# One core, three stages: q and k transposed by 64x64 products, one engine for the transposed x, and one-column result rows

## The chip, the cores and the metric

The kernel runs on one core of one Trainium2 chip. Its time is the device's time of one execution in microseconds (us); lower is better. Beside plain runs there is one profiled execution, from which the trace comes.

## The reference

Three computations follow each other. Everything is float32.

```python
# 1. attention in chunks of 64: batch 8, heads 8, sequence 576, head size 64
scores = (1 / sqrt(64)) * q_c @ k_c.T          # 64x64 per chunk and head
attn   = exp(scores - max); attn /= (sum + 1e-9)
x      = attn @ v_c                            # as 4608 tokens of 512
# 2. one expert of 8 for each token, chosen by normalized x against the experts' embeddings
logits = xn @ en.T / tau;  e = argmax(logits);  gate = softmax(logits)[e]
x      = gate * (relu(x @ w1[e]) @ w2[e])      # 512 -> 1024 -> 512
# 3. a gated layer
h = x @ w_in;  out = (h * sigmoid(1.702 * h)) @ w_out    # 512 -> 2048 -> 512
```

## The kernel before

The order of the work is written out by hand: each engine runs its instructions in the order in which the program issues them, and waits are put in where data or a buffer is needed. There is no planner.

**Attention loop.** 36 tiles of 128 tokens. `n` counts iterations (loop near the end of the first half, up to `n = 38`), and the stages of one tile are spread over several iterations. q and k are loaded by SyncE in units of 256 tokens (`load_qk`, 18 units, five buffers for k and four for q); v comes in 64 loads with three buffers of a batch each. In iteration n, in this order: `emit_T` transposes one unit of k or q on TensorE and returns the copies from PSUM to SBUF, which ScalarE makes; ScalarE squares x of tile n-3 (`emit_sq`); TensorE transposes the 16-bit pair of x of tile n-5 (`emit_XT`), forms the scores of tile n (`emit_S`); VectorE takes their maximum and subtracts it (`max_S`); `evac_XT` copies the transposed x out of PSUM, by ScalarE for odd tiles and from tile 30 on, by VectorE for the other even ones; `emit_X` forms the 16-bit pair of x of tile n-3 in one of three buffers, and SyncE stores it to `xs`; then come the transposed weights (`emit_PT`), the product with v (`emit_PV`) of tile n-2, the exponential (`exp_S`) and the division (`emit_x`). Between these, `drip(1)` issues one more VectorE step of the gate of an earlier batch of tiles (`norm`, `gate`, `order`, `tables`), and the logits of an earlier tile go ahead of the scores. The stores to `xs` and the loads of q, k and v stand in one queue, SyncE's, in the order of the program.

**Gate and slots.** The gate's last batch ends after the loop. `order` finds the tokens of the first three slots of 128 tokens, `tables` and `find_tokens`, `find_scales` those of all. `scale_of` builds each token's scale as the bits of a float (`sc_i`) from three looked-up parts.

**Experts.** 39 slots of 128 tokens: gather (`fetch`), DMA transpose (`turn`), `mm1` with a relu that ScalarE (high half) and VectorE (low half) make, `mm2`, then `mm2_evac`. At a change of expert `swap` splits new weights on ScalarE and VectorE; `load_next` loads the next ones. In the order of each engine `mm2_evac` of a slot follows the swap of w2, and the relu of the next slot follows it. `mm2_evac` squares the result on ScalarE with the sum per row, and VectorE makes from the sum a power of two that brings the row into the range of a 16-bit pair, and joins it with the token's scale; ScalarE then writes the high half of y, VectorE the low half, and four 32-bit words behind each row carry the token's number twice and its scale twice. Beside it `big_split` prepares the weights of stage 3 on VectorE, ScalarE and GpSimd.

**Gated layer.** Nine groups of 512 tokens, from about 672 us to the end; the diff does not touch it.

Of the kernel before, what the change touches and what calls it, by code (L numbers as in the profile page):

```python
# [9 lines left out]
F32 = mybir.dt.float32  # L10
F16 = mybir.dt.float16
BF16 = mybir.dt.bfloat16
I32 = mybir.dt.int32
U32 = mybir.dt.uint32
AF = mybir.ActivationFunctionType
ALU = mybir.AluOpType
# [8 lines left out]
BIAS = 127  # L25
# [3 lines left out]
EXP_BITS = 0x7F800000  # L29
MAN_BITS = 0x007FFFFF  # L30
# [4 lines left out]
def kernel(  # L35
# [13 lines left out]
    nc = tc.nc  # L49
    B, H, S, D = q.shape  # L50
    NT, DM = out.shape
# [4 lines left out]
    HP = H // 2  # L56
# [5 lines left out]
    MAXT = NTILE + NE - 1  # L62
# [7 lines left out]
    const = ctx.enter_context(tc.tile_pool(name="const", bufs=1))  # L70
# [4 lines left out]
    ps = ctx.enter_context(tc.tile_pool(name="ps", bufs=1, space=PSUM))  # L75
# [9 lines left out]
    YP = 2 * DM + 8  # L85
# [9 lines left out]
    identF = const.tile([128, 128], F32, name="identF")  # L95
# [5 lines left out]
    QR = QU // 128  # L101
# [27 lines left out]
    for b in range(B):  # L129
        for h in range(H):  # L130
            hp, h2 = divmod(h, 2)
# [20 lines left out]
    for t in vt:  # L152
# [15 lines left out]
        out=tri16, in_=ones16, pattern=[[1, 128]], compare_op=ALU.is_gt, fill=0.0,  # L168
# [19 lines left out]
    for m_, op_ in ((lt_m, ALU.is_lt), (le_m, ALU.is_le)):  # L188
        nc.vector.tensor_tensor(
            out=m_, in0=io_e.unsqueeze(1).to_broadcast([128, NE, NE]),  # L190
            in1=io_e.unsqueeze(2).to_broadcast([128, NE, NE]), op=op_,
# [15 lines left out]
    )  # L207
    id_i = const.tile([128, MAXT], I32, name="id_i")
    sc_i = const.tile([128, MAXT], I32, name="sc_i")

    tau_sb = const.tile([128, 1], F32, name="tau_sb")
    nc.scalar.dma_start(out=tau_sb, in_=tau.partition_broadcast(128))
# [121 lines left out]
    qkT = {}  # L334

    def emit_T(u, nm):

        src = raw.pop((u, nm))
        qkT[u, nm] = att.tile([128, HP, QU], F32, tag=nm + "T", name=nm + "T", bufs=2)
        evacs = []  # L340
        for h2 in range(2):
            p = ps.tile([128, HP, 128], F32, tag="A", name="tp", bufs=2)
            for hp in range(HP):
                nc.tensor.transpose(  # L344
                    p[:, hp, :], src[:, 2 * hp + h2].rearrange("p r d -> p (r d)"), identF
                )
            dst = qkT[u, nm][h2 * 64:(h2 + 1) * 64].rearrange("p hp (c r) -> p hp r c", r=QR)
            evacs.append([
                lambda r=r, p=p, dst=dst: nc.scalar.activation(  # L349
                    out=dst[:, :, r], in_=p[r * 64:(r + 1) * 64], func=AF.Copy  # L350
                )
                for r in range(2)
            ])
        return evacs

# [6 lines left out]
    xtp = sp2[:, :, HP * CH:512].bitcast(F16).rearrange("p a (c k) -> p a c k", k=128)  # L362
# [107 lines left out]
    def evac_XT(t):  # L470
        xT = att.tile([128, 2 * KD, 128], F16, tag="xTa", name="xTa", bufs=2)
        xv = xT.rearrange("p (a c) k -> p a c k", a=2)
        if t >= 30 or t % 2:
            nc.scalar.activation(out=xv, in_=xtp, func=AF.Copy)
        else:
            nc.vector.tensor_copy(xv, xtp)
        xT_t[t] = xT

    batches = [(0, 8), (8, 8), (16, 8), (24, 6), (30, 6)]
# [65 lines left out]
    def scale_of(cols, got, parts_i):  # L545
        nc.vector.tensor_copy(parts_i[:, 0], got[:, 0])
        nc.vector.scalar_tensor_tensor(
            out=parts_i[:, 1], in0=got[:, 1], scalar=1024.0, in1=got[:, 2], op0=ALU.mult, op1=ALU.add
        )
        nc.vector.scalar_tensor_tensor(  # L550
            out=sc_i[:, cols], in0=parts_i[:, 0], scalar=21, in1=parts_i[:, 1],
            op0=ALU.logical_shift_left, op1=ALU.bitwise_or
        )

    def gate(bi):
# [327 lines left out]
    def reg(ap, engines, hi):  # L883
        return nc.values_load(ap, engines=engines, min_val=0, max_val=hi)
# [163 lines left out]
    def mm2(i):  # L1048
        mm2_part(i, 0, KF)
        mm2_evac(i)  # L1050
# [15 lines left out]
    def mm2_evac(i):  # L1066
        hT_t.pop(i)
        p = py_t.pop(i)
        y = mo.tile([128, YP], F16, tag="y", name="y", bufs=2)
        ysq = mo.tile([128, DM], F16, tag="ysq", name="ysq", bufs=1)  # L1070
        s = mo.tile([128, 4], F32, tag="ys", name="ysc", bufs=2)
        si = s.bitcast(I32)
        c_i = sc_i[:, i:i + 1]
        tail = y[:, 2 * DM:YP].bitcast(I32).rearrange("p (a two) -> p a two", two=2)
        n = (YP - 2 * DM) // 4
        nc.scalar.activation(out=ysq, in_=p, func=AF.Square, scale=2.0 ** -20, accum_out=s[:, 0:1])
        nc.vector.tensor_scalar(si[:, 3:4], c_i, EXP_BITS, None, op0=ALU.bitwise_and)
        nc.vector.tensor_copy(tail[:, :, 0], id_i[:, i:i + 1].to_broadcast([128, n]))
        nc.vector.tensor_scalar(s[:, 0:1], s[:, 0:1], Y_MIN * 2.0 ** -40, None, op0=ALU.max)
        nc.vector.tensor_scalar(  # L1080
            si[:, 1:2], si[:, 0:1], 24, 23, op0=ALU.logical_shift_right, op1=ALU.logical_shift_left
        )
        nc.vector.tensor_scalar(
            si[:, 1:2], si[:, 1:2], -1.0, float((BIAS + Y_TOP - 20) << 23), op0=ALU.mult, op1=ALU.add
        )
        nc.vector.scalar_tensor_tensor(  # L1086
            out=si[:, 2:3], in0=c_i, scalar=MAN_BITS, in1=si[:, 1:2], op0=ALU.bitwise_and, op1=ALU.bitwise_or
        )
        nc.scalar.activation(out=y[:, 0:DM], in_=p, func=AF.Copy, scale=s[:, 2:3])  # L1089
        nc.vector.scalar_tensor_tensor(  # L1090
            out=y[:, DM:2 * DM], in0=p, scalar=s[:, 2:3], in1=y[:, 0:DM], op0=ALU.mult, op1=ALU.subtract
        )
        nc.vector.scalar_tensor_tensor(
            out=tail[:, :, 1], in0=si[:, 3:4].to_broadcast([128, n]), scalar=float(BIAS << 23),
            in1=si[:, 1:2].to_broadcast([128, n]), op0=ALU.add, op1=ALU.subtract,
        )
        if i < NSURE:
            nc.sync.dma_start(out=ys[i * 128:(i + 1) * 128, :], in_=y)
        elif i < SURE:
            row = reg(idx_y[0:1, i:i + 1], [ENG.SP], NT)  # L1100
            nc.sync.dma_start(out=ys[bass.ds(row, 128), :], in_=y)
        else:
            nc.gpsimd.indirect_dma_start(
                out=ys[:, :], out_offset=bass.IndirectOffsetOnAxis(ap=idx_y[:, i:i + 1], axis=0),
                in_=y[:, :], in_offset=None,
            )
# [8 lines left out]
    for nm in ("ku", "qu"):  # L1115
        for e in emit_T(0, nm):
            for f in e:
                f()
# [24 lines left out]
    for n in range(NTILE + 3):  # L1143
        rate[0] = 2 if 29 <= n < 33 else 1
        u, step = n // QR + 1, n % QR
        ev = [[], []]
        if u < NQ:
            ev = emit_T(u, "ku" if step == 0 else "qu")
            load(2 if n in (5, 9, 13, 17) else 1)
# [8 lines left out]
        if n - 1 in back:  # L1158
            evac_XT(back[n - 1])
            turned.append(back[n - 1])  # L1160
# [4 lines left out]
        if n in front:  # L1165
            evac_XT(front[n])
            turned.append(front[n])
# [31 lines left out]
        if n == NTILE + 2:  # L1199
            evac_XT(NTILE - 1)  # L1200
# [26 lines left out]
    swap(NSURE, 1)  # L1227
    steps(99)
    mm2_evac(1)
    turn(4)  # L1230
    fetch(5)
# [609 lines left out]
```

## Time and profile before

| | |
|---|---|
| runs | 1352.38, 1353.53, 1356.58 us; median 1353.53 |
| profiled execution | 1351.38 us, span 1349.4 us, mean granted clock 0.976 |
| TensorE (PE) busy | 1246.7 us (92%) |
| VectorE (DVE) busy | 1048.0 us (78%) |
| ScalarE (ACT) busy | 732.8 us (54%) |
| GpSimd (POOL) busy | 718.4 us (53%) |

The page divides the span into 40 slices of 33.7 us; a digit is the busy share in tenths, and PEclk the clock that TensorE was granted, in tenths:

```profile
PE   6777767899999999999899999999999999999997
DVE  4688888878988778886678696968687896968681
ACT  7899855235544545554463645545454645455452
PEclk9999877999999999999999999999999999999999
DMA  9999635668665759885507162544526062534413
```

The attention loop fills the first six or seven slices, the experts those up to the twentieth, the gated layer the rest. Busy shares are means over stages with different limits. "L349" is line 349 of the kernel; "<-" in a row's brackets tells what ended the wait ahead of it. PEld is TensorE's weight load, which runs beside its products.

### The profile page before, as it was taken

The page shows a single profiled execution, that of the slowest core. Times are in us where ns is not written, and L with a number is a line of the kernel's source. Part 1 is how long each engine was busy: PE and PEld are TensorE (multiplying, and loading weights), DVE is VectorE, ACT ScalarE, POOL GpSimd, SP SyncE. Part 2 cuts the span into 40 slices and gives each one's busy share as a digit, 9 for nine tenths or more (in the row PEclk, how much of TensorE's full clock was granted, in tenths as well). Part 3 has the DMA queues.
Part 4 walks back from the last instruction along what each step waited for, and adds up shares of the span by engine and source line. Part 5 has one row for each costly group of instructions (what it writes and reads, how often), then busy time and mean ns, then how long its engine had stood idle before and what let it go on. Part 6 is the DMA issues. An engine that isn't in the chain of part 4 may idle for free. (4 is left out here: it accounts for less than half of the span.)

```text
span 1349.4 us, 35343 instructions
## 1 busy us (share of the span) xinstructions
PE 1246.7 (92%) x14192; PEld 1027.2 (76%) x14192; DVE 1048.0 (78%) x1872; ACT 732.8 (54%) x1301; POOL 718.4 (53%) x652
## 2 busy tenths in 40 slices
PE   6777767899999999999899999999999999999997
PEld 4666656677676666667588888888888888888886
DVE  4688888878988778886678696968687896968681
ACT  7899855235544545554463645545454645455452
POOL 1455543142444254543167575757667675757664
PEclk9999877999999999999999999999999999999999
DMA  9999635668665759885507162544526062534413
GB/s 197 233 242 230 160 129 131 181 181 229 191 182 174 212 161 274 266 253 133 151 15 212 58 183 99 129 154 94 188 39 226 19 205 77 157 125 125 157 42 116
DMA packets 218454, 213.62 MB, mean 158 GB/s; under 512 B 127320, under 2 KB 171352, under 8 KB 218272
## 3 DMA queue, kind: packets, MB, share of 16 engines
q1 hardware_dynamic: 204880, 184.17, 51.0%
q0 software_dynamic: 6000, 19.67, 4.3%
q10 hardware_dynamic: 7392, 7.36, 1.6%
q8 instruction: 114, 1.87, 0.6%
q14 instruction: 68, 0.56, 0.2%
HBM read 154.98 MB, written 36.52 MB: 142 GB/s over the span
## 5 line engine op out<-in xcount | busy, mean ns | idle before, releaser
L1536 PEld LDWEIGHTS <-wS 128*128 128x128 f16 x3024 | 296.2, 98 | 48.9 <-issue 9.7
L1029 PEld LDWEIGHTS <-w1HL 128*128 128x128 f16 x3744 | 216.9, 99 | 24.1 <-DVEq L962 6.7
L1029 PE MATMUL ph<-xTm,w1HL 128*128 128x128 f16 x3744 | 223.0, 222 | 12.2 <-DVEq L962 5.5
L1064 PE MATMUL py<-w2HL,hT 128*128 128x512 f16 x912 | 203.9, 379 | 6.0 <-DVEq L962 3.4
L1064 PEld LDWEIGHTS <-hT 128*128 128x128 f16 x936 | 89.9, 98 | 109.1 <-issue 8.0
L1089 ACT ACTIVATE y<-py,ysc 128x512 f16<-128x512 f32 x38 | 26.1, 687 | 142.8 <-DVE ysc L1086 142.8
L1004 POOL DMA_INDIRECT xg<-xs,id_i x39 | 44.3, 1135 | 107.6 <-DMA xTm<-xg 70.0
L1536 PEld LDWEIGHTS <-w2HL 128*128 128x128 f16 x864 | 84.6, 98 | 10.6
L1536 PEld LDWEIGHTS <-w1HL 128*128 128x128 f16 x864 | 84.5, 98 | 9.8
L454 POOL TENSOR_TENSOR x<-x,sx_all 128x512 f32<-128x512 f32 x33 | 34.3, 1039 | 107.3 <-DVE rd L424 41.9
L1256 POOL TENSOR_TENSOR wS<-d_f,wS 128x512 f16<-128x512 f32 x28 | 37.0, 1339 | 73.4 <-ACT wS L1255 44.5
L1562 ACT ACTIVATE zA<-zA 128x512 f32<-128x512 f32 x72 | 45.3, 628 | 53.2 <-DVE zA L1559 26.9
L1403 POOL TENSOR_TENSOR w1HL<-zA,w1HL 128x512 f16<-128x512 f32 x36 | 48.5, 1346 | 43.6 <-ACT w1HL L1399 39.7
L1396 DVE TENSOR_TENSOR zA<-zA 128x512 f32<-128x512 f32 x72 | 65.6, 910 | 1.2
L1037 DVE SCALAR_TENSOR_TENSOR hT<-ph,hT 128x512 f16<-128x512 f32 x78 | 51.4, 684 | 14.8 <-ACT hT L1036 14.7
L1036 ACT ACTIVATE hT<-ph 128x512 f16<-128x512 f32 x78 | 44.2, 594 | 30.0 <-PE ph L1029 30.0
L1536 PE MATMUL pd<-stg,wS 128*128 128x256 f16 x456 | 54.5, 272 | 2.2 <-ACT stgB L1399 2.2
L1697 POOL DMA_INDIRECT out_dram<-hT,idc x36 | 35.4, 983 | 35.7 <-ACT hT L1692 32.6
L1536 PE MATMUL pa<-stg,wS 128*128 128x256 f16 x432 | 51.7, 273 | 1.5 <-ACT stgB L1399 1.5
L1090 DVE SCALAR_TENSOR_TENSOR y<-py,ysc,y 128x512 f16<-128x512 f32 x38 | 28.5, 751 | 28.8 <-ACT y L1089 28.8
L1536 PE MATMUL pb<-stg,wS 128*128 128x256 f16 x408 | 48.9, 272 | 1.5 <-ACT stgB L1399 1.5
L349 ACT ACTIVATE kuT<-tp 64x512 f32<-64x512 f32 x72 | 45.2, 628 | 8.8 <-PE tp L344 7.9
(408 smaller groups left out, 3134.4 us busy)
## 6 DMA issues: line engine op xcount, KB each, us to landing
ring<-wod SPq DMA_DIRECT2D x63, 1024.0 KB, 5.1
stg<-in_moe_w_dram SPq DMA_DIRECT2D x14, 1024.0 KB, 6.9
stgB<-in_moe_w_dram SPq DMA_DIRECT2D x14, 1024.0 KB, 6.8
ys<-y SPq DMA_DIRECT2D x39, 258.0 KB, 3.2
vt<-in_v_dram SPq DMA_DIRECT2D x64, 144.0 KB, 5.7
xs<-xr SPq DMA_DIRECT2D x36, 256.0 KB, 5.6
raw_o<-in_moe_w_in_dram SPq DMA_DIRECT2D x16, 512.0 KB, 4.3
raw_o<-in_moe_w_out_dram SPq DMA_DIRECT2D x16, 512.0 KB, 3.8
```

What stands on the lines that cost most here:

```text
L349: lambda r=r, p=p, dst=dst: nc.scalar.activation(out=dst[:, :, r], in_=p[r * 64:(r + 1) * 64], func=AF.Copy)
L1004: nc.gpsimd.indirect_dma_start(out=xg[:, :], out_offset=None, in_=src, in_offset=bass.IndirectOffsetOnAxis(ap=id_i[:, i:i + 1], axis=0),)
L1029: nc.tensor.matmul(p[:, f % 4], wt[:, c, fs], xT[:, a, :], start=(c == 0 and a == 0 and wt is w1H), stop=(c == KD - 1 and wt is w1L),)
L1036: nc.scalar.activation(out=hi, in_=p, func=AF.Relu)
L1037: nc.vector.scalar_tensor_tensor(out=lo, in0=p, scalar=0.0, in1=hi, op0=ALU.max, op1=ALU.subtract)
L1064: nc.tensor.matmul(p, hT[:, a, :], wt[:, c, :], start=st, stop=sp)
L1256: nc.gpsimd.tensor_tensor(out=L_, in0=f, in1=H_, op=ALU.subtract)
L1396: nc.vector.tensor_tensor(out=o, in0=x, in1=p, op=op)
L1403: eng.tensor_tensor(out=lo, in0=x, in1=hi, op=ALU.subtract)
L1536: nc.tensor.matmul(dst, lhs(a, k, ab), rhs(b, k), start=first and ab == abs_[0] and k == 0 and m == 0, stop=(k == n - 1 and m == 2), skip_ ...
L1562: nc.scalar.activation(out=z, in_=z, func=AF.Sigmoid, scale=1.702 * 2.0 ** -G_EXP)
L1697: disjoint("out", nc.gpsimd.indirect_dma_start(out=out[:, :], out_offset=bass.IndirectOffsetOnAxis(ap=id_t[j][0][:, 2 * h + t, 0:1], axis= ...
```

## The change

Four edits. `emit_T` no longer transposes 128x128 blocks (two rows of 64 channels side by side) but multiplies 64x64 blocks by a 64x64 identity, so that both heads of a pair land at the partitions where they are wanted; two copies of 128 partitions take the place of four of 64 (the PSUM side is read with a step). `evac_XT` uses ScalarE for every tile. `scale_of` also makes the scale's mantissa as a float (`sc_m`) and its exponent part (`sc_e`). `mm2_evac` writes the four words behind a row with four one-column tensor-scalar operations, takes the exponent from `sc_e`, and multiplies `sc_m` instead of joining bits.

```diff
--- before.py
+++ after.py
@@ -207,6 +207,8 @@
     )
     id_i = const.tile([128, MAXT], I32, name="id_i")
     sc_i = const.tile([128, MAXT], I32, name="sc_i")
+    sc_m = const.tile([128, MAXT], I32, name="sc_m")
+    sc_e = const.tile([128, MAXT], F32, name="sc_e")
 
     tau_sb = const.tile([128, 1], F32, name="tau_sb")
     nc.scalar.dma_start(out=tau_sb, in_=tau.partition_broadcast(128))
@@ -338,18 +340,22 @@
         src = raw.pop((u, nm))
         qkT[u, nm] = att.tile([128, HP, QU], F32, tag=nm + "T", name=nm + "T", bufs=2)
         evacs = []
-        for h2 in range(2):
-            p = ps.tile([128, HP, 128], F32, tag="A", name="tp", bufs=2)
-            for hp in range(HP):
-                nc.tensor.transpose(
-                    p[:, hp, :], src[:, 2 * hp + h2].rearrange("p r d -> p (r d)"), identF
+        p = [ps.tile([128, QR, HP, 64], F32, tag="A", name="tp", bufs=2) for _ in range(2)]
+        for hp in range(HP):
+            for r in range(QR):
+                for a in range(2):
+                    rows = slice(a * 64, (a + 1) * 64)
+                    for h2 in range(2):
+                        nc.tensor.matmul(
+                            p[a][h2 * 64:(h2 + 1) * 64, r, hp, :], src[rows, 2 * hp + h2, r, :],
+                            identF[rows, rows], start=True, stop=True,
+                        )
+        for a in range(2):
+            dst = qkT[u, nm][:, :, a * 128:(a + 1) * 128].rearrange("p hp (i r) -> p hp i r", r=QR)
+            evacs.append([
+                lambda a=a, dst=dst: nc.scalar.activation(
+                    out=dst, in_=p[a].rearrange("p r hp i -> p hp i r"), func=AF.Copy
                 )
-            dst = qkT[u, nm][h2 * 64:(h2 + 1) * 64].rearrange("p hp (c r) -> p hp r c", r=QR)
-            evacs.append([
-                lambda r=r, p=p, dst=dst: nc.scalar.activation(
-                    out=dst[:, :, r], in_=p[r * 64:(r + 1) * 64], func=AF.Copy
-                )
-                for r in range(2)
             ])
         return evacs
 
@@ -470,10 +476,7 @@
     def evac_XT(t):
         xT = att.tile([128, 2 * KD, 128], F16, tag="xTa", name="xTa", bufs=2)
         xv = xT.rearrange("p (a c) k -> p a c k", a=2)
-        if t >= 30 or t % 2:
-            nc.scalar.activation(out=xv, in_=xtp, func=AF.Copy)
-        else:
-            nc.vector.tensor_copy(xv, xtp)
+        nc.scalar.activation(out=xv, in_=xtp, func=AF.Copy)
         xT_t[t] = xT
 
     batches = [(0, 8), (8, 8), (16, 8), (24, 6), (30, 6)]
@@ -550,6 +553,13 @@
         nc.vector.scalar_tensor_tensor(
             out=sc_i[:, cols], in0=parts_i[:, 0], scalar=21, in1=parts_i[:, 1],
             op0=ALU.logical_shift_left, op1=ALU.bitwise_or
+        )
+        nc.vector.tensor_scalar(
+            sc_m[:, cols], sc_i[:, cols], MAN_BITS, BIAS << 23, op0=ALU.bitwise_and, op1=ALU.bitwise_or
+        )
+        nc.vector.tensor_scalar(sc_e[:, cols].bitcast(I32), sc_i[:, cols], EXP_BITS, None, op0=ALU.bitwise_and)
+        nc.vector.tensor_scalar(
+            sc_e[:, cols], sc_e[:, cols].bitcast(I32), float(BIAS << 23), None, op0=ALU.add
         )
 
     def gate(bi):
@@ -1070,12 +1080,10 @@
         ysq = mo.tile([128, DM], F16, tag="ysq", name="ysq", bufs=1)
         s = mo.tile([128, 4], F32, tag="ys", name="ysc", bufs=2)
         si = s.bitcast(I32)
-        c_i = sc_i[:, i:i + 1]
-        tail = y[:, 2 * DM:YP].bitcast(I32).rearrange("p (a two) -> p a two", two=2)
-        n = (YP - 2 * DM) // 4
+        tail = y[:, 2 * DM:YP].bitcast(I32)
         nc.scalar.activation(out=ysq, in_=p, func=AF.Square, scale=2.0 ** -20, accum_out=s[:, 0:1])
-        nc.vector.tensor_scalar(si[:, 3:4], c_i, EXP_BITS, None, op0=ALU.bitwise_and)
-        nc.vector.tensor_copy(tail[:, :, 0], id_i[:, i:i + 1].to_broadcast([128, n]))
+        for a in range(0, tail.shape[1], 2):
+            nc.vector.tensor_scalar(tail[:, a:a + 1], id_i[:, i:i + 1], 0, None, op0=ALU.bitwise_or)
         nc.vector.tensor_scalar(s[:, 0:1], s[:, 0:1], Y_MIN * 2.0 ** -40, None, op0=ALU.max)
         nc.vector.tensor_scalar(
             si[:, 1:2], si[:, 0:1], 24, 23, op0=ALU.logical_shift_right, op1=ALU.logical_shift_left
@@ -1083,17 +1091,15 @@
         nc.vector.tensor_scalar(
             si[:, 1:2], si[:, 1:2], -1.0, float((BIAS + Y_TOP - 20) << 23), op0=ALU.mult, op1=ALU.add
         )
-        nc.vector.scalar_tensor_tensor(
-            out=si[:, 2:3], in0=c_i, scalar=MAN_BITS, in1=si[:, 1:2], op0=ALU.bitwise_and, op1=ALU.bitwise_or
-        )
+        nc.vector.tensor_scalar(s[:, 2:3], s[:, 1:2], sc_m[:, i:i + 1].bitcast(F32), None, op0=ALU.mult)
         nc.scalar.activation(out=y[:, 0:DM], in_=p, func=AF.Copy, scale=s[:, 2:3])
         nc.vector.scalar_tensor_tensor(
             out=y[:, DM:2 * DM], in0=p, scalar=s[:, 2:3], in1=y[:, 0:DM], op0=ALU.mult, op1=ALU.subtract
         )
-        nc.vector.scalar_tensor_tensor(
-            out=tail[:, :, 1], in0=si[:, 3:4].to_broadcast([128, n]), scalar=float(BIAS << 23),
-            in1=si[:, 1:2].to_broadcast([128, n]), op0=ALU.add, op1=ALU.subtract,
-        )
+        for a in range(1, tail.shape[1], 2):
+            nc.vector.tensor_scalar(
+                tail[:, a:a + 1], si[:, 1:2], -1.0, sc_e[:, i:i + 1], op0=ALU.mult, op1=ALU.add
+            )
         if i < NSURE:
             nc.sync.dma_start(out=ys[i * 128:(i + 1) * 128, :], in_=y)
         elif i < SURE:
```

## Rows read from the trace of the kernel before

**Rows 1.** Busy time by stretch, microseconds from the span's start; the columns stand first.

```profile
core 0: us, PE busy (x) PEld busy (x) DVE busy (x) ACT busy (x) POOL busy (x), PEclk, DMA share, GB/s
60.00:135.00 75.00, 58.16 (x1401) 46.77 (x1402) 64.84 (x210) 70.33 (x131) 42.47 (x46) 1.00 1.13 235
135.00:157.00 22.00, 17.06 (x419) 13.53 (x418) 19.45 (x58) 21.34 (x40) 11.38 (x11) 1.00 0.93 220
157.00:225.00 68.00, 45.35 (x868) 39.39 (x868) 56.78 (x193) 41.40 (x77) 29.26 (x31) 0.70 0.40 125
...
267.00:672.00 405.00, 389.76 (x4304) 282.76 (x4301) 327.85 (x561) 196.02 (x337) 162.97 (x136) 0.99 0.70 203
```

**Rows 2.** Groups by line, ScalarE, 60:135: busy, mean ns, idle before.

```profile
L349 ACT ACTIVATE kuT<-tp 64x512 f32<-64x512 f32 x32 | 20.1, 628 | 0.4
L349 ACT ACTIVATE quT<-tp 64x512 f32<-64x512 f32 x29 | 18.2, 628 | 0.4
...
L474 ACT ACTIVATE xTa<-sp 128x1024 f16<-128x1024 f16 x8 | 8.2, 1024 | 0.3
```

**Rows 3.** Groups by line, VectorE, 60:135.

```profile
L452 DVE TENSOR_SCALAR xr<-x,sx_all 128x512 f16<-128x512 f32 x15 | 7.2, 481 | 4.7 <-DMA xs<-xr 4.6
L476 DVE COPY xTa<-sp 128x1024 f16<-128x1024 f16 x8 | 5.4, 681 | 0.0
```

**Rows 4.** DMA issues, 60:135: count, KB each, median us to landing.

```profile
xs<-xr SPq DMA_DIRECT2D x15, 256.0 KB, 6.5
```

**Rows 5.** DMA issues, 155:190.

```profile
xs<-xr SPq DMA_DIRECT2D x5, 256.0 KB, 2.0
```

**Rows 6.** Timeline of TensorE: start, us, what, [idle before].

```profile
106.67 0.69 PE L371 MATMUL sp<-kuT,quT 64*64 64x64 f32 x32
...
166.85 1.09 PE L344 MATMUL tp<-identF,qu 128*128 128x128 f32 x8
...
178.62 1.75 PE L344 MATMUL tp<-identF,ku 128*128 128x128 f32 x7
...
198.80 1.13 PE L371 MATMUL sp<-kuT,quT 64*64 64x64 f32 x32
```

**Rows 7.** Timeline of VectorE, 157:160.

```profile
157.91 0.68 DVE L476 COPY xTa<-sp 128x1024 f16<-128x1024 f16 x1
158.51 0.21 DVE L572 TENSOR_TENSOR g_l<-g_l,g_mx 128x64 f32<-128x64 f32 x1
```

**Rows 8.** Waits of VectorE, 157:225: total, times, longest.

```profile
DVE mx L378 <- PE sp L371: 5.0, 3, 2.7
```

**Rows 9.** Timeline, 264:268.

```profile
265.08 0.26 DVE L550 SCALAR_TENSOR_TENSOR sc_i<-got2i 128x40 int32<-128x40 int32 x1
...
265.26 1.27 DVE L1037 SCALAR_TENSOR_TENSOR hT<-ph,hT 128x512 f16<-128x512 f32 x2
...
266.65 1.66 PE L1029 MATMUL ph<-xTm,w1HL 128*128 128x128 f16 x21 [1.65 <-DVEq L962]
```

**Rows 10.** Three lines of mm2_evac, whole span: ns min/median/max.

```profile
L1078 DVE COPY y<-id_i x39: 153/159/4056, 242.0 to 661.6; 128x2 int32<-128x2 int32 x39
...
L1080 DVE TENSOR_SCALAR ysc<-ysc x39: 153/154/155, 242.2 to 665.3; 128x1 int32<-128x1 int32 x39
...
L1086 DVE SCALAR_TENSOR_TENSOR ysc<-sc_i,ysc x39: 159/159/2114, 242.6 to 665.7; 128x1 int32<-128x1 int32 x39
```

**Rows 11.** Timeline, 551:557, and one copy at 596.

```profile
551.97 0.14 DVE L1077 TENSOR_SCALAR ysc<-sc_i 128x1 int32<-128x1 int32 x1
552.03 0.62 DVE L1078 COPY y<-id_i 128x2 int32<-128x2 int32 x1
...
553.12 0.32 DVE L1086 SCALAR_TENSOR_TENSOR ysc<-sc_i,ysc 128x1 int32<-128x1 int32 x1
...
555.24 0.29 PE L1029 MATMUL ph<-xTm,w1HL 128*128 128x128 f16 x2 [1.91 <-ACTq L962]
...
596.63 0.62 DVE L1078 COPY y<-id_i 128x2 int32<-128x2 int32 x1
```

## The prediction

> **What bounds the kernel now.** I read the page first (busy shares, the 40 slices), then busy time by stretch, then groups by line, waits and the timeline inside the stretches that the diff touches. From 267 us on, TensorE is busy 389.8 of 405.0 us, and the page's 40 slices show it full to the end: edits on other engines can win back only its 15.2 us of idle time there [rows 1]. The attention loop (36 tiles, up to about 225 us) is another matter: from 60 to 135 us ScalarE is busy 70.3 of 75.0 us, VectorE 64.8, TensorE 58.2, and the transfers have a busy share of 1.13 at 235 GB/s [rows 1]. Two things are full at once there, ScalarE and the transfers. That the transfers really queue is seen at the store of x: 6.5 us from issue to landing in this stretch, 2.0 us once the loads are through [rows 4, 5]; and VectorE waits 4.6 us for such a store before it may write the next x pair [rows 3]. The loads of q, k and v don't shrink with the change, and stores and loads stand in one queue in the order of the program, so the loop can't run more than its three x buffers ahead of them. From 135 to 157 us the transfers fade out (share 0.93) and ScalarE is busy 21.3 of 22.0 us [rows 1]. [...]
>
> **The change part by part.**
>
> *Copies of transposed q and k.* 144 copies of 64x512 become 72 of 128x512. One takes 628 ns at 64 partitions [rows 2]. No row shows a ScalarE copy that reads PSUM with a step of 256 elements, as the new one does. From below: it is as long as a contiguous one of the same 512 elements, 0.63 us; from above: twice that, 1.25 us, as if the two halves went one after the other. I take 0.63, the nearest row having the same count of elements per partition and a step on its output side. In 60 to 135 us the 61 copies hold 38.3 us [rows 2]; half goes: 19.2 us.
>
> *x copied by ScalarE alone.* 8 VectorE copies of 0.68 us (5.4 us) [rows 3] become 8 ScalarE copies of 1.02 us (8.2 us) [rows 2] in that stretch. ScalarE then has 70.3 - 19.2 + 8.2 = 59.3 us of work, VectorE 64.8 - 5.4 = 59.4 us.
>
> *64x64 products in place of transposes.* Per call of emit_T 8 transposes (1.09 us at the full clock) go, and 32 products come, which the trace counts twice each in this type (two passes), so 64 entries. The score products have the same shape, type and order over the four quadrants: 32 entries take 0.69 us at the full clock, 1.13 us at the lower level [rows 6]. 64 take 1.38 and 2.26 us. The transposes at the lower level: 7 take 1.75 us [rows 6], 8 some 2.0. So +0.3 us per call at either level; below: 0 (entries overlap at the seam), above: 2.76 us per call if only two quadrants ran at a time, +1.7. In 60 to 135 us, 15 calls add 4.5 us: TensorE 62.7 of 75. Its first products now wait for both PSUM buffers, where half of the transposes could start with one; behind them in TensorE's queue stand the logits, the transposes of x and the scores, and VectorE waits for those. In the loop's fullest stretch TensorE keeps 12 us to spare, so I cost that wait at nothing; were the cover gone, it is the 0.3 us a call again.
>
> [...]
>
> *One-column rows of y.* Per tile four operations go (the masking of the exponent, a two-column copy, a scalar-tensor-tensor of one column and one of two) and five one-column tensor-scalar operations come: two stay ahead of the sum of squares, one takes the place of the scale step, and behind the low half of y stand two instead of one. The copy's median is 159 ns, its longest 4056; the old scale step 159 and 2114; a one-column tensor-scalar is 153 to 155 ns in all 39 cases [rows 10]. So VectorE gains time where it was held, but that counts only where TensorE waits behind it. One such place, whole: copy 0.62 us, scale step 0.32, then y and hT on ScalarE, then TensorE's first product of the next tile after 1.91 us idle [rows 11]. Without the holds, 0.46 + 0.16 = 0.62 us. I find one more (copy 0.62 us at 596.6 us [rows 11]): 0.46. The other holds end while TensorE has work. Against it, an added row ahead of hT, 0.06 us from one start to the next [rows 11], at the 7 expert changes that 8 experts make: 0.4 us. Net -0.7 us; bounds -4 (a quarter of the 15.2 us) and +1.
>
> *scale_of* gets three more operations per call. The second call stands ahead of hT of tile 3, and TensorE waits 1.65 us behind that: the 40-column word at 265.08, hT 0.18 us later, then TensorE at 266.65 [rows 9]. Three more of 0.2 us each: +0.6 us (bounds 0 and 0.8). The first call (3 columns) is followed by a wait of VectorE for scores, 2.7 us at the longest [rows 8]: +0.2.
>
> **The sum, by stretch.** 0 to 135 us: ScalarE gets 11.0 us lighter, but the transfers have the same bytes at the same rate; what ScalarE frees turns into longer waits of VectorE for the stores of x, and of TensorE behind that. I take 0; bounds -10 and 0. 135 to 157 us (five iterations): 10 copies of 0.63 go, some 2.5 copies of 1.02 come, -3.7 us for ScalarE, -1.7 for VectorE, and the last loads take part of it back: -2.0; bounds -3.7 and 0. 157 to 225 us: three VectorE copies (tiles 24, 26, 28) stand in VectorE's chain of gate work: 157.91 to the next start at 158.51, 0.60 us each [rows 7], -1.8; two calls of emit_T stand ahead of scores that VectorE waits for, +0.6; scale_of +0.2: -1.0. 225 to 267 us: +0.6. 267 to 672 us: -0.7. After that nothing is touched: 0. Sum -3.1 us. The profiled execution took 1351.38 us (span 1349.4 and 2.0 around it), so 1348.3 on its own scale; the median of the runs, 1353.53, lies 2.15 above it: 1350.4 us.
>
> **The rivals.** (A) *The transfers keep up.* If a loop that asks sooner is served sooner, the fullest engine sets the time: TensorE's 62.7 us at the 94% that ScalarE reaches now is 66.9 us for 75.0: -8, with the -3.1 above 1342.4 us. For it: 235 GB/s is a mean, and ScalarE's 94% leaves little visible waiting for the transfers. Against: store landings of 6.5 against 2.0 us.
> (B) *The wide copy doesn't do what it says* (slower side). Place: ScalarE in 60 to 157 us. Price: at 1.25 us a copy nothing is saved and the 8.2 us come on top: 78.5 us of ScalarE, at 94% 83.5 us, +8.5, and +2.5 in the next 22 us: 1364 us. It decides from 0.99 us a copy (70.3 - 38.3 + 8.2 + 30.5 x 0.99 = 70.3).
> (C) *Only two quadrants work at a time*: 2.76 us a call, TensorE 58.2 + 15 x 1.67 = 83 us for 75, with its waits 1365 to 1370 us; decides from 2.2 us a call. Against: the score products.
> (D) *The clock.* In 157 to 225 us TensorE falls to the lower level after idle stretches, and VectorE waits three times, 5.0 us in all, for scores that come late [rows 8]. If plain products hold the level up where transposes do not, up to those 5.0 us come back: about -4, 1346.5 us. Against: at 60 to 135 us the granted clock is 1.00 with the transposes [rows 1]. [...]
>
> **How the numbers follow.** Forecast 0.60, own range 1346 to 1354.5 us; A 0.17, B 0.10, C 0.06, D 0.07. A measurement of this kernel can tell 0.3%, about 4.1 us, from no change, so the line is at 1349.5, one us below the forecast: of the forecast's 0.60 some 0.20 lie beyond it, 0.38 within, 0.02 above. Faster: 0.20 + 0.17 + 0.06 = 0.43. Same: 0.38 + 0.01 = 0.39. Slower: 0.02 + 0.10 + 0.06 = 0.18. The range takes in A's full bound (-10, with part of the rest) and most of B: 1340 to 1362 us.
>
> **What would show it.** Right: copies of 128x512 near 0.63 us, 72 of them; 64 entries per call in about 1.4 us; ScalarE's busy time in 60 to 135 us down by some 10 us with the stretch no shorter, and VectorE's wait for stores of x longer than 4.6 us; the one-column rows never above 0.16 us; TensorE's wait near 266 us longer by 0.6. Wrong: over 15 tiles in 60 to 135 us (A), copies near 1 us (B), calls over 2 us (C), a granted clock in 157 to 225 us well over 0.70 (D). A gain of more than 2 us after 267 us would show that I mis-sized the held rows.

## The result: slower by 0.8%, and where TensorE stopped

The changed kernel took 1364.96 us (median of 7 runs) beside 1354.98 us of the kernel before: ratio 1.0081, 95% interval 1.0060 to 1.0101. The forecast was 1350.4 us with a range up to 1362. In the profiled executions the span went from 1349.4 to 1363.2 us, and all of that and more arose in the attention loop: VectorE's maximum over the last tile's scores starts at 216.21 us, before at 200.83, 15.4 us later. Behind the loop 1.5 us come back.

The page of the changed kernel (busy time by engine, four rows of the 40 slices, the queue that carries instructions; that queue's row on the page of the kernel before stands last, by itself):

```profile
span 1363.2 us, 39339 instructions
...
PE 1254.5 (92%) x16208; PEld 1041.4 (76%) x16208; DVE 1018.0 (75%) x1902; ACT 697.5 (51%) x1244; POOL 718.7 (53%) x652
...
ACT  3666656235543545454464555545464645555453
POOL 1344544224453344453157575766767675757664
PEclk9889977989999999999999999999999999999999
DMA  9999616285684859878606253452617162534413
...
q8 instruction: 129, 2.11, 0.7%
```

```profile
q8 instruction: 114, 1.87, 0.6%
```

ScalarE's first five slices fell from 7 to 9 tenths to 3 to 6, and TensorE's clock is down to 8 tenths in the second, third and ninth. Busy time by stretch; the last row is the stretch of the experts, shifted by the 15 us that the loop lost:

```profile
core 0: us, PE busy (x) PEld busy (x) DVE busy (x) ACT busy (x) POOL busy (x), PEclk, DMA share, GB/s
60.00:135.00 75.00, 56.64 (x1978) 48.38 (x1970) 53.69 (x175) 50.55 (x96) 34.81 (x36) 0.91 1.03 221
135.00:157.00 22.00, 16.74 (x596) 14.27 (x592) 13.49 (x45) 12.89 (x26) 12.11 (x15) 0.92 0.63 164
157.00:225.00 68.00, 46.69 (x1417) 39.82 (x1410) 57.35 (x189) 43.51 (x82) 32.99 (x33) 0.79 0.45 133
282.00:687.00 405.00, 390.76 (x4307) 283.98 (x4307) 305.32 (x599) 197.30 (x337) 163.40 (x136) 0.99 0.71 203
```

Beside [rows 1]: from 60 to 135 us ScalarE has 50.6 us of work in place of 70.3, VectorE 53.7 in place of 64.8, the transfers' share is 1.03 in place of 1.13, and still fewer tiles go through. No engine is full: the fullest, TensorE, is busy 56.6 of 75 us. What the engines wait for tells more. TensorE's waits from 20 to 160 us, first the kernel before, then the changed one (what waited, what ended the wait: total us, times, longest):

```profile
PE tp L344 <- ACT quT L349: 8.7, 11, 0.8
PE tp L344 <- ACT kuT L349: 7.3, 10, 1.1
```

```profile
PE tp L349 <- issue: 12.4, 10, 2.2
PE db L422 <- issue: 7.9, 5, 2.1
PE sp L377 <- issue: 5.7, 5, 2.8
...
PE ptp L400 <- issue: 2.1, 1, 2.1
```

Before, TensorE's largest waits there were for ScalarE's copies. Now it waits for "issue", that is, for nothing that the profile links to it: no tile, no semaphore, no engine, and in front of four different kinds of work. The timeline of one such stop, in the middle of 32 products of one kind (PT, which they read, had been written by 75.27 us):

```profile
77.62 0.33 PE L422 MATMUL db<-vt,PT 64*64 64x65 f32 x4
79.76 0.62 PE L422 MATMUL db<-vt,PT 64*64 64x65 f32 x26 [1.81 <-issue]
```

and the queues in the 1.2 us around its beginning (77.2 to 78.4 us; packets, MB, share):

```profile
q1 hardware_dynamic: 866, 0.32, 114.7%
q8 instruction: 1, 0.02, 5.5%
```

One packet of 16 KB of the queue of kind "instruction" runs there, from 77.28 to 78.34 us, and TensorE goes on 1.42 us after it ends. Two counts of my own on the trace's rows show what this is. First, the page has 129 packets of that queue (2.11 MB, 16 KB each) and had 114 (1.87 MB) before; TensorE's rows (products, weight loads, waits) went from 28,560 to 32,554. That is one packet per 250 to 252 rows before and after; with the step of 256 found below, the queue carries TensorE's instructions, 256 of them in 16 KB. Second, number TensorE's rows from the first, and take each pause over 60 ns up to 300 us that ends by "issue":

```
kernel    pauses by "issue"   sum us   row number modulo 256
before            1             3.3    15
changed          27            31.0    193, all 27 of them
```

These stops all fall on the same row modulo 256, whatever the work there is: I read them as the ends of 16 KB blocks of instructions whose successor has not come. In the 24 stopped blocks from 26 to 165 us the packet of the next block starts 1.0 to 3.8 us (median 2.3) after the block before it began to execute, lasts 0.9 to 1.6 us, and the first of its instructions runs 1.1 to 1.7 us (median 1.4) after its end. The two medians and the 1.1 us that a packet takes in the median make 4.8 us, my estimate of what a block of 256 instructions needs there in the median; the 29 block beginnings in that stretch lie 3.42 to 6.47 us apart, median 4.8. The kernel before is supplied in the same way, one block ahead: from 20 to 165 us its packets start at most 3.6 us after the beginning of the former block (median 1.7; one starts 0.65 us ahead of it), but a block lasts 4.9 to 11.0 us, and the packet has ended 1.7 to 7.5 us before the first of its instructions runs. A tile of the kernel before has 184 TensorE rows (8 transposes of q or k, 32 entries of score products, 32 of value products, 4, 8 and 8 others, each with its weight load), 256 of them in 6.8 us at its 4.9 us a tile. The changed one has 296 a tile, 256 in 4.2 us at that pace.

### The profile page after: what moved, and what is told of

Its sections match the earlier page's. It is cut to its first block, busy times and chain, and to the rows that moved or that the text cites. A ratio compares the mean times of both kernels' runs of the same rounds, so it can differ in the third digit from the quotient of the medians.

```text
span 1363.2 us, 39339 instructions
## 1 busy us (share of the span) xinstructions
PE 1254.5 (92%) x16208; PEld 1041.4 (76%) x16208; DVE 1018.0 (75%) x1902; ACT 697.5 (51%) x1244; POOL 718.7 (53%) x652
## 3 DMA queue, kind: packets, MB, share of 16 engines
q8 instruction: 129, 2.11, 0.7%
## 5 line engine op out<-in xcount | busy, mean ns | idle before, releaser
L1262 POOL TENSOR_TENSOR wS<-d_f,wS 128x512 f16<-128x512 f32 x28 | 37.7, 1363 | 79.9 <-ACT wS L1261 44.5
L384 DVE TENSOR_REDUCE mx<-sp 128x8 f32<-128x512 f32 x36 | 24.8, 690 | 55.1 <-PE sp L377 53.7
L479 ACT ACTIVATE xTa<-sp 128x1024 f16<-128x1024 f16 x36 | 36.8, 1023 | 44.2 <-DVE si_all L448 17.5
```

The lines of the kernel that those rows point to most:

```text
L1262: nc.gpsimd.tensor_tensor(out=L_, in0=f, in1=H_, op=ALU.subtract)
```

## The experiments

Where loads are left out or q and k are cut, the expectation says so. "Stops" are pauses by "issue" at row 193 modulo 256 up to 300 us, "loop" is the start of the last tile's maximum against 200.8 us of the kernel before, both from the one profiled execution. That execution lies up to 4.4 us from the median of its runs (3.5 above it in number 14, 4.4 below it in 13), so loops that differ by less than some 4 us are not told apart here.

**1. The first part alone.** The kernel before with the changed emit_T:

```diff
-                nc.tensor.transpose(
-                    p[:, hp, :], src[:, 2 * hp + h2].rearrange("p r d -> p (r d)"), identF
-                )
+                        nc.tensor.matmul(
+                            p[a][h2 * 64:(h2 + 1) * 64, r, hp, :], src[rows, 2 * hp + h2, r, :],
+                            identF[rows, rows], start=True, stop=True,
+                        )
...
```

> The kernel before with the first part of the change alone: q and k by 64x64 products and 128-partition copies. Theory (TensorE's instruction stream): the trace of the changed kernel shows TensorE standing still 0.7 to 2.8 us, 31 us in all up to 300 us, always at the same place of its instruction stream modulo 256, after a 16 KB transfer of the queue of kind instruction; the products add 112 instructions a call, and that is the whole loss: 1366 to 1370 us, with the same stops. Rival (x copied by ScalarE alone, or the one-column rows, bring the loss): 1350 to 1357 us.

1371.11 us, ratio 1.0109 (1.0089 to 1.0128); 25 stops, 32.4 us, all at 193; loop +23.7 us, in an execution 3.0 us above the median. The products carry the whole loss, a little more than was forecast.

**2. The changed kernel without it.** The reverse diff.

> The changed kernel with the first part undone: 128x128 transposes and 64-partition copies again, x copied by ScalarE alone and the one-column rows kept. Theory: no stop of TensorE at the ends of instruction blocks; ScalarE, 70.3 of 75.0 us before, gets 8.2 us more between 60 and 135 us, so the attention loop is 3 to 8 us longer than before, the part behind it 1 us shorter: 1356 to 1362 us. Rival (the loss isn't the products): about 1365 us.

1350.98 us, ratio 0.9969 (0.9952 to 0.9985): faster than the kernel before. No stops; loop +0.7. The expected cost of x on ScalarE (3 to 8 us of loop) did not come, although ScalarE is busy 73.95 of 75.0 us from 60 to 135: with x off VectorE, the loop is as long as before.

**3 and 4. Instructions or TensorE's time?** Both start from the kernel before; 3 puts the loop ahead of each group of four transposes.

```diff
+            for _ in range(28):
+                nc.tensor.matmul(
+                    p[0:64, 0, 0:1], ident16[0:64, 0:64], ident16[0:64, 0:1], start=True, stop=True
+                )
```

```diff
-            for hp in range(HP):
+            for hp in [*range(HP), *range(HP)]:
                 nc.tensor.transpose(
```

> The kernel before with 56 products of 64x64 f16 by one column ahead of each call's transposes, into the PSUM that these then write over: 112 more TensorE instructions a call, as many as the change adds, and about 1.2 us of its time by the score products' 0.69 us for 32 entries. Nothing else is changed. Theory (instruction stream): stops at the same place modulo 256 between 20 and 160 us, loop 12 to 25 us longer: 1366 to 1380 us. Rival (TensorE's time is what counts): as in the kernel with twice the transposes, which adds 1.1 us a call with 16 instructions.

> The kernel before with every transpose of q and k done twice into the same place: 1.09 us more of TensorE a call with 16 more instructions. Theory (instruction stream): no stops at the ends of blocks, TensorE 58.2 + 16 of 75.0 us between 60 and 135 us, so 0 to 8 us longer: 1354 to 1362 us. Rival (TensorE's time counts): as long as the kernel with small products.

Number 4: 1353.99 us, ratio 0.9991 (0.9977 to 1.0005). TensorE is busy 68.8 us of the 75 in place of 58.2, and it costs nothing that the runs can tell (loop +2.6 in the one execution): TensorE's time in the loop was as free as the prediction said. From 60 to 135 us:

```profile
60.00:135.00 75.00, 68.83 (x1516) 59.09 (x1515) 64.64 (x209) 69.57 (x129) 41.48 (x45) 1.00 1.17 239
```

Number 3: 1414.52 us, 1.0450, but it does not answer the question as put. It has almost no stops (0.4 us). 28 of those products, each into the same PSUM word, take 1.02 us at the full clock, not the 0.6 that I had worked out, and TensorE is simply full:

```profile
60.00:135.00 75.00, 74.96 (x1767) 66.91 (x1770) 47.63 (x141) 55.07 (x100) 31.01 (x32) 0.84 0.74 184
```

At its pace of 6.5 us a tile the refill keeps up with as many instructions as the changed kernel has. This speaks for the rate and against the number.

**5 and 6. Are the transfers to blame?** The changed kernel and the kernel before, both with 40 of the 64 loads of v left out:

```diff
         while vq and v_n[0] < upto:
             dst, src = vq.popleft()
+            if v_n[0] >= NV * H:
+                v_n[0] += 1
+                continue
```

> The changed kernel with the loads of v left out beyond the first three batches (40 of 64 loads of 144 KB; those batches' v is used again in their place). Same instructions on TensorE. Theory (its instruction stream comes late because the transfers are full): the transfers have room, the stops at the ends of blocks fall from 31 us to under 10 us, and the attention loop ends 12 to 25 us earlier than in the changed kernel: 1340 to 1353 us. Rival (the stops come of the number of instructions alone, whatever the transfers do): stops of some 30 us as before, 1362 to 1367 us.

> The kernel before with the same 40 loads of v left out. If the loop before was bound by transfers, as the prediction said for 0 to 135 us, some 6 of its 38 MB go and it ends 10 to 20 us earlier: 1335 to 1345 us. If ScalarE (70.3 of 75.0 us) bound it, 0 to 4 us earlier: 1350 to 1355 us.

Number 5: 1356.92 us, ratio 1.0023 to before, loop +11.5, where I had expected 1340 to 1353 us and under 10 us of stops; the share of the transfers from 60 to 135 us falls from 1.03 to 0.63, the stops only from 31.0 to 25.2 us:

```profile
60.00:135.00 75.00, 60.00 (x2090) 51.59 (x2082) 54.75 (x176) 50.73 (x97) 35.15 (x36) 0.89 0.63 171
```

I had thought that the block waits in a queue behind the loads; that is the smaller part of it. What else holds the packet back 1 to 3.8 us stays open. Number 6: 1351.53 us, ratio 0.9975 (0.9959 to 0.9990), loop -0.9 us: the loop of the kernel before was not bound by transfers alone.

**7. Half of the instructions, everything else as changed.**

```diff
+        high = src.bitcast(BF16).rearrange("p h r (d two) -> p h r d two", two=2)[:, :, :, :, 1]
...
-                            p[a][h2 * 64:(h2 + 1) * 64, r, hp, :], src[rows, 2 * hp + h2, r, :],
-                            identF[rows, rows], start=True, stop=True,
+                            p[a][h2 * 64:(h2 + 1) * 64, r, hp, :], high[rows, 2 * hp + h2, r, :],
+                            identB[rows, rows], start=True, stop=True,
```

> The changed kernel with the same 64x64 products, PSUM buffers and 128-partition copies, but q and k read as the upper halves of their words (bf16) against a bf16 identity: q and k are cut to bf16, and a product takes one pass, so a call issues 64 instructions on TensorE in place of 128 (16 in the kernel before). Theory (instruction stream): stops at the ends of blocks under 8 us in place of 31, 1343 to 1354 us. Rival (the small products' waits for both PSUM buffers, or the wide copies, hold the loop): 1360 us or more.

1346.09 us, ratio 0.9933 (0.9909 to 0.9957), 8 stops of 6.1 us in all, loop -1.7. The PSUM buffers, the quadrants, the order and the wide copies are those of the changed kernel; with 64 instructions a call in place of 128 the loss of 10 us becomes a gain of 8. The loop goes from +15.4 to -1.7 us; against the kernel before another 4.0 us of the one execution are won behind the loop, and these are not explained. The clock is not the loss either: from 60 to 135 us it is 0.74 here, lower than the changed kernel's 0.91. (The one-pass products are shorter, too: with them TensorE is busy an estimated 3.4 us a tile, from the 55.25 us for 1914 entries in number 11, 116 a tile, in place of 4.1, both at a granted clock of 0.91. That TensorE's time is not what counts, number 4 had shown.)

**8. The one-column rows alone**, all lines of the change in mm2_evac and scale_of.

```diff
-        nc.vector.tensor_copy(tail[:, :, 0], id_i[:, i:i + 1].to_broadcast([128, n]))
+        for a in range(0, tail.shape[1], 2):
+            nc.vector.tensor_scalar(tail[:, a:a + 1], id_i[:, i:i + 1], 0, None, op0=ALU.bitwise_or)
...
```

> The kernel before with the last part of the change alone: one-column rows of y and the longer scale_of; q, k and x as before. The changed kernel with the transposes back gained 3.6 us. If the one-column rows bring that, by the freed VectorE between 267 and 672 us: 1350 to 1352 us, attention loop as before. Rival (it comes of ScalarE copying x alone): 1353 to 1355 us.

1351.50 us, ratio 0.9977 (0.9964 to 0.9990). This overlaps with number 2 (0.9969), so x on ScalarE, with the old transposes, is worth nothing that can be told over the whole run. The one profiled execution is 0.3 us longer than before, with a loop 1.6 us longer, so it can't place the gain.

**9 and 13. The products beside the old transposes.** The changed kernel's 32 products go into the same PSUM, ahead of the transposes that write over them; 9 in full float32, 13 on bf16 halves in one pass. Four transposes a PSUM buffer and two copies follow as before.

```diff
+        p = [ps.tile([128, QR, HP, 64], F32, tag="A", name="tp", bufs=2) for _ in range(2)]
...
         for h2 in range(2):
-            p = ps.tile([128, HP, 128], F32, tag="A", name="tp", bufs=2)
+            tp = p[h2].rearrange("p r hp i -> p (r hp i)").rearrange("p (hp c) -> p hp c", c=128)
...
```

> The kernel before with the change's 64x64 products issued ahead of the transposes, into the same PSUM, which the transposes then write over; copies, x and rows as before. TensorE gets 128 more instructions a call and 1.4 us more of work (the kernel with twice the transposes had 1.1 us more and cost nothing). Theory (instruction stream): stops of 25 to 45 us at one place modulo 256, loop 18 to 35 us longer, 1370 to 1388 us. Rival (TensorE's time, or the wide copies, made the loss): 1353 to 1360 us.

> The kernel before with the change's small products issued ahead of the transposes as before (their results are written over, so q and k stay exact), but as one-pass bf16 products: 64 more TensorE instructions a call in place of 128, with the same waits for both PSUM buffers, the same order and the old copies. Products beside the transposes in full float32 cost 33 us, of which only 15.5 us stand as stops. If instructions are the rest too (a late refill delays a tile's first copy, and ScalarE behind it): under 1365 us, stops under 8 us. If the wait for both PSUM buffers, emptied by four half copies, is the rest: 1368 us or more, with TensorE waiting for ScalarE's copies.

Number 9: 1387.61 us, ratio 1.0247, loop +37.1, but 15.5 us of stops, fewer than expected. Number 13: 1365.02 us, ratio 1.0078 (1.0059 to 1.0097), stops 6.3, loop +7.3, at the edge of what was expected. Halving the instructions (and, by the estimate under number 7, taking some 0.7 us off the products of a call) takes back 22.6 of 33 us; the remaining 10 us are not told apart (TensorE waits 16.2 us for ScalarE's copies between 20 and 160 us, 16.0 in the kernel before). In 9 the visible stops are less than half of the loss, so stops don't add up to a loss one for one; the split of its other half is not settled.

**10. Products for q alone**, k by transposes.

> The changed kernel with k transposed and copied as before the change, q alone by products: 18 of the 36 calls. Theory (instruction stream): half of the added instructions, and since only a rate above what the refill gives stops TensorE, less than half of the stops (5 to 13 us in place of 31); ScalarE saves half of its copies: 1346 to 1357 us, and under the changed kernel's time in any case. Rival (each call of products costs its own 0.4 us): half of the loss, 1359 to 1361 us.

1349.99 us, ratio 0.9972 (0.9955 to 0.9988), 12 stops of 11.0 us: half of the added instructions, a third of the stops, and the loss is gone.

**11. Number 7 with the loads of v left out as in 5 and 6.**

> The kernel with one-pass products (q and k cut to bf16, 6 us of stops left, ScalarE 55 of 75 us) with the 40 loads of v beyond the first three batches left out as well. Relieving the transfers alone gave 2.5 us, relieving ScalarE alone 2 us in the loop. If both were full at once, as the prediction said, relieving both gives more than the sum: the attention loop 10 to 20 us shorter, 1328 to 1340 us. Rival (a third thing bounds the loop next, such as the refill of the instruction stream or the chain of one tile): within 4 us of the one-pass kernel, 1342 to 1347 us.

1336.93 us, ratio 0.9874 (0.9852 to 0.9896), 6.6 us of stops, loop -10.0 us. Relieving the transfers alone (6) gave 0.9 us in the loop, ScalarE alone (7) 1.7, both 10.0, each from one execution. By the medians of the runs it is 0.25% and 0.67% against 1.26%: more than the sum, but by 0.34%, which the three intervals do not clear; and a part of 11's gain lies behind the loop, where other values of x go to the experts. From 60 to 135 us, numbers 6, 7 and 11:

```profile
60.00:135.00 75.00, 59.08 (x1414) 47.22 (x1406) 67.12 (x215) 71.50 (x134) 43.19 (x46) 1.00 0.73 192
```

```profile
60.00:135.00 75.00, 60.00 (x1758) 49.45 (x1758) 58.96 (x195) 54.76 (x106) 40.66 (x45) 0.74 1.13 241
```

```profile
60.00:135.00 75.00, 55.25 (x1914) 45.39 (x1902) 63.74 (x209) 59.16 (x115) 45.01 (x48) 0.91 0.71 196
```

In the first ScalarE is full (71.5 of 75) and the transfers are not (0.73), in the second the transfers are (1.13) and ScalarE is not, in the third neither. VectorE's wait for stores of x, 4.6 us there before, is 5.8 us in 7 and does not appear in 6 and 11. So two things were full at once: the rows show it, the sum of the gains agrees without proving it.

**12 and 14. Exact products with half of the instructions.** All 128 rows and 128 moving columns in one product, full float32; 12 for q alone with k by transposes, 14 for both; each of a call's two PSUM buffers is copied whole, 128x512 (the lines of 12, inside a loop over r; 14 has the same ones for both):

```diff
...
+                p = ps.tile([128, HP, 128], F32, tag="A", name="tp", bufs=2)
+                for hp in range(HP):
                     for h2 in range(2):
                         nc.tensor.matmul(
...
+                            p[h2 * 64:(h2 + 1) * 64, hp, :], src[:, 2 * hp + h2, r, :], identF,
+                            start=True, stop=True,
                         )
+                dst = qkT[u, nm].rearrange("p hp (c r) -> p hp r c", r=QR)[:, :, r]
...
```

> The changed kernel with k transposed and copied as before, and q by 16 products a call of 128 rows, 64 columns of weights and 128 moving columns in full float32 (64 TensorE instructions a call in place of 128), copied at 128 partitions. Theory (instruction stream): stops under 4 us (one-pass products with 64 instructions in every call had 6). By the score products a product of a quarter of the size takes 21.6 ns when four run at once, so 32 entries of four times the size are some 2.7 us a call, 1.1 us more than with quadrants in every second call; twice the transposes showed that 1.1 us a call is free: 1345 to 1351 us, under both kernels. Rival (these products fill TensorE): 1354 to 1362 us.

> The changed kernel with q and k both by the tall products (128 rows, 64 columns of weights, 128 moving columns, full float32, 64 TensorE instructions a call), copied at 128 partitions. With q alone that way a call took 2.1 us and TensorE was busy 66.5 of 75.0 us from 60 to 135 us; k that way adds some 8 x 1.1 us, 75 of 75. Theory (instruction stream): stops under 7 us, and the loop is set by TensorE: 1346 to 1356 us, slower than with q alone. Rival (ScalarE's relief counts more than TensorE's load): 1338 to 1345 us.

Number 12: 1345.89 us, ratio 0.9940 (0.9921 to 0.9959), 1.9 us of stops, loop -6.1: faster than both kernels, with q and k exact. Number 14: 1349.49 us, ratio 0.9959 (0.9943 to 0.9976), 5.3 us of stops, loop +1.1 in an execution 3.5 us above the median. It has the changed kernel's rows and x and makes every call by products that last longer, with half of the instructions: some 15 us faster than the change by the medians. From 60 to 135 us, 12 and then 14:

```profile
60.00:135.00 75.00, 66.50 (x1660) 54.75 (x1661) 61.90 (x202) 69.16 (x129) 44.50 (x48) 1.00 1.14 243
```

```profile
60.00:135.00 75.00, 70.78 (x1786) 61.08 (x1780) 61.78 (x205) 57.70 (x108) 42.02 (x46) 1.00 1.13 241
```

In 14 TensorE (70.8 of 75) is the fullest engine, as ScalarE (70.3) was before. In 12 a call of q takes 2.1 us (17.1 us for 256 entries, 32 a call) and still fits.

## Why the prediction was wrong

**The step that failed** is "In the loop's fullest stretch TensorE keeps 12 us to spare, so I cost that wait at nothing", in the part on the products, and with it the term "0 to 135 us: I take 0; bounds -10 and 0" of the sum. That term measured +18.3 us: the 25th tile's maximum starts at 150.7 us, before at 132.5. The wait named in that step, for both PSUM buffers, did cost next to nothing (TensorE waits 0.5 us for copies from 60 to 135 us, before 10.7); the spare time itself was gone. I priced a product by its duration, and that price was good: calls of 64 entries that no stop breaks took 1.1 to 1.3 us at the full clock (predicted 1.38) and 1.9 to 2.0 where it was low (2.26). TensorE's time was free too (number 4). What I did not price is that each product also brings a weight load, and the trace counts both twice: 64 rows of products and 64 of weight loads, 128 instructions a call in place of 16, and that these have to be brought in. The page showed the queue that does it, 114 packets before, and I read past it. My upper bound for the products (2.76 us a call, quadrants by twos) was a bound on execution, and none of the rivals B to D was about supply. From 60 to 135 us the changed kernel passes 13.7 tiles (877 entries of tp, 64 each), before 15.25 (61 copies, four each): 5.47 us a tile in place of 4.92. Of that TensorE is busy 4.13 (3.81 before: the +0.3 as predicted) and stands 1.34 (1.10 before); 15.4 us of its 18.4 us idle are stops at block ends. Before, 10.7 us of its waits were for ScalarE's copies, slack behind the fuller engine. Now its own work (56.6 us) and the stops fill 72.0 of the 75 us.

**Right in mechanism:** the 0 for the first 135 us, as far as ScalarE's relief goes: with the stops mostly gone (7), the 25th tile's maximum starts at 133.8 us, before at 132.5, and VectorE waits 5.8 us for stores of x in place of 4.6. The reason given, transfers and ScalarE full together, is borne out by the rows of 6, 7 and 11. Rival A, "the transfers keep up", got no support: alone, ScalarE's relief gave 1.7 us of loop.

**The other steps**, in rows of the changed kernel:

```profile
L356 ACT ACTIVATE kuT<-tp x36: 577/597/607, 8.3 to 198.7; 128x512 f32<-128x512 f32 x36
L356 ACT ACTIVATE quT<-tp x36: 576/597/607, 11.3 to 205.0; 128x512 f32<-128x512 f32 x36
```

```profile
171.41 1.27 PE L349 MATMUL tp<-identF,qu 64*64 64x64 f32 x64 [0.74 <-ACT kuT L356]
```

```profile
L458 DVE TENSOR_SCALAR xr<-x,sx_all 128x512 f16<-128x512 f32 x14 | 7.0, 499 | 0.3
```

The wide copy takes 0.60 us (0.63 forecast), so rival B is out, and C with the 1.27 us. In the changed kernel VectorE's wait for stores of x did not grow beyond 4.6 us [rows 3]; it went, and VectorE waits 14.4 us for scores there instead. From the 30th tile's maximum to the last one's it took 42.0 us, before 44.5: -2.5 where I had -1.0. This is not D: between these two maxima the granted clock is 0.72, before 0.71 (the 0.79 in the row above for 157 to 225 us holds 17 us of the stage before), and the products alone (1) take 43.9 us, the rows alone (8) 44.5, but the old transposes with x on ScalarE (2) 41.6. The gain goes with x off VectorE, which I had put at -1.8; each of these is one execution, and the difference is small. What D says of falls after idle stretches is in the trace of before: the granted clock is 1.00 or 0.50 in all its records, and from 157 to 225 us it falls at 158.3, 172.0, 192.4 and 219.7 us, each time in a stretch of 1.7 to 6.0 us in which TensorE has no work, or some 1.5 us behind one. That transposes and plain products differ in this, no run shows.

The rows of y (ns min/median/max):

```profile
L1086 DVE TENSOR_SCALAR y<-id_i x78: 137/146/155, 257.3 to 676.7; 128x1 int32<-128x1 int32 x78
```

```profile
L1094 DVE TENSOR_SCALAR ysc<-ysc,sc_m x39: 213/214/215, 258.0 to 680.8; 128x1 f32<-128x1 f32 x39
```

```profile
L1100 DVE TENSOR_SCALAR y<-ysc,sc_e x78: 202/205/208, 259.6 to 682.5; 128x1 int32<-128x1 int32 x78
```

None is held any more (the longest is 215 ns, before 4056 and 2114 [rows 10]), but those with a scalar from a tile take 0.21 us, not up to 0.16. TensorE's idle time in the 405 us of the experts is 14.2 us, 15.2 before [rows 1]; number 8, the rows with the longer scale_of, timed 0.23% faster, some 3 us (interval 1.4 to 4.9), where the forecast's three terms for it (-0.7, +0.6, +0.2) make +0.1. By the prediction's own sign the held rows were mis-sized, if that gain lies behind the loop, which no profile shows. The second scale_of:

```profile
281.81 1.28 DVE L1047 SCALAR_TENSOR_TENSOR hT<-ph,hT 128x512 f16<-128x512 f32 x2
...
283.20 0.50 PE L1039 MATMUL ph<-xTm,w1HL 128*128 128x128 f16 x3 [2.60 <-DVEq L972]
```

TensorE waits 2.60 us there, 1.65 before [rows 9]: +0.95, forecast +0.6.

## What to carry to other kernels

Count instructions beside durations: where an edit trades a few long TensorE instructions for many short ones, work out how many microseconds 256 of them last in the stage concerned and compare that with the refill seen in the trace (here some 4.8 us a block in the median). Pauses by "issue" in front of all kinds of work, all at one row number modulo 256, were the sign here (27 of them, 31.0 us). Here a form with fewer and longer instructions, on an engine that had time to spare, won over one that is shorter by duration (14, 1349.49 us, against the change, 1364.96; 12, with q alone, was the fastest of those with exact q and k).

## What the runs showed of the hardware

- In the changed kernel TensorE stopped 27 times up to 300 us, 31.0 us in all, each time at row 193 modulo 256; from 26 to 165 us the next 16 KB packet ended 1.1 to 1.7 us ahead of the first row that ran again (24 stops), and the beginnings of blocks lay 3.4 to 6.5 us apart. In the kernel before, whose blocks lasted 4.9 to 11.0 us from 20 to 165 us, no pause by "issue" fell on row 193. With the share of the transfers at 0.63 in place of 1.03 (5) the stops were still 25.2 us.
- The next block's packet starts after the beginning of the block before it or at most 0.65 us ahead of it, in both kernels (median 1.7 us after it before the change, 2.2 after the change, 20 to 165 us): one block ahead, not several.
- A granted clock of 0.74 from 60 to 135 us (7) went with a loop no longer than before: TensorE, busy 60.0 of the 75 us, did not set the pace there.
- 28 products of 64x64 by one column into one PSUM word take 1.02 us at the full clock (3), 36 ns each, where the quadrants' score products pass at 21.6 ns an entry [rows 6].
